# A fixed order of steps, engines and buffer slots in place of a planner, and a last batch cut into two token halves

## The chip, the cores and the metric

The kernel runs on one core of one Trainium2 chip. The metric is the time of one execution on the device in microseconds (us), smaller is better; the number compared is the median of several runs.

## What is computed

Two layers in a row, both attention. The first works on 4 batches of 8 heads with 768 tokens of 64 values: every token sees its neighbours closer than 16 tokens and a summary of each of the 24 blocks of 32 tokens (largest key, mean value). Its output, 4 batches of 768 tokens by 512 values, goes into four expert heads with causal attention; each token keeps its two best experts.

```python
# first layer, per batch and head
k_sum = k.reshape(B, H, nb, block, D).max(axis=3)
v_sum = v.reshape(B, H, nb, block, D).mean(axis=3)
scores_all = concat([where(|i - j| < 16, scale*q@k.T, -1e9), scale*q@k_sum.T + log(32)])
a = softmax(scores_all);  x = a @ concat([v, v_sum])
# second layer, per batch
logits = x @ w_gate;  topk = 2 best of 4;  w = softmax of the two
for e in range(4):
    q, k, v = x @ wq[e], x @ wk[e], x @ wv[e]
    a = softmax(causal(scale * q @ k.T))
    out += (e in topk) * w_e * (a @ v @ wo[e])
```

## The kernel before

A batch and two heads make a **pair**; there are 16, four to a batch. `stage1_pair` loads q, k and v of a pair, narrows q and k to 16 bits (`narrow`), turns them on TensorE (`turn`, `take`), takes the largest key of each block (`key_sums`), fills the value tile (`overlap`, `fill_rows`) and then does two halves of 384 tokens each: `scores`, `expo` (the exponential), `values`, `recip` and `norm`, `back` (turned back) and `take_hi`, `take_lo`, which keep the result as a 16-bit number and its remainder. The block means of v come from one more load for each batch (`load_vs`, tile `v_s`, 1536 KB), four additions that halve it each time (`fold`), a trip through DRAM (`park`, `fetch`) and one addition (`join`); no `values` of a batch can run before its `join`.

When the four pairs of a batch are done, `values_and_gate` makes the experts' values and the gate (`gate_a`, `gate_b`, `gate_exp`, `gate_c`), `experts(b, cc)` does two experts at a time: two projections, six units of scores with their exponentials, the causal cut on GpSimd (`causal`), the weighing in two parts (tokens 0 to 2 and 3 to 5, counted in tiles of 128), then `recip`, `comb`, `scale`, `turn` and `keep_t` for all six token tiles at once. `output` projects two token tiles at a time, copies them out of PSUM (`keep`) and stores them through GpSimd's queue (`store`).

Each such step is declared once with an engine (or several that could do it) and a cost. The order is not the order of declaration: `Plan.schedule` places step after step on the engine that can start one first, in the order of a priority made of a base time and an offset from the table `PO`, and hands out buffer slots as they come free. The emitted program is that order, and every engine works through its own list strictly in order. So a step that waits holds everything behind it on its engine, and SyncE, which issues all loads, holds all later loads while one waits for its slot.

Slots matter: two tiles each for the loaded q and k (`q_f`, `k_f`), three value tiles (`v_blk`), one `v_s`, two staging tiles for weights (`w_st`); in PSUM two tiles of one bank (`P1`) and three of two banks (`P2`).

Of the kernel before, what the change touches and what calls it, by code (L numbers as in the profile page):

```python
# [64 lines left out]
PO = {  # L65
    'const_ident': -11.677,
    'const_idt': 1.577,
    'const_mask': 33.311,
    'const_pads': 7.266,
    'experts.causal': 8.585,  # L70
    'experts.comb': -19.049,
    'experts.expo': -5.527,
    'experts.keep': 11.958,
    'experts.keep_t': 2.062,
    'experts.project': -0.122,
    'experts.recip': -4.407,
    'experts.scale': 11.954,
    'experts.scores': 4.304,
    'experts.turn': 18.467,
    'experts.weigh.go': 7.812,  # L80
    'output.keep': 15.877,
    'output.project': -32.546,
    'output.store': 2.114,
    'stage1_pair.back': -3.094,
    'stage1_pair.expo': -0.092,
    'stage1_pair.fetch': -2.828,
    'stage1_pair.fill_rows.go': 10.985,
    'stage1_pair.fold': 6.215,
    'stage1_pair.join': -10.17,
    'stage1_pair.key_sums': 5.122,  # L90
    'stage1_pair.load.go': 0.943,
    'stage1_pair.load_v': -0.911,
    'stage1_pair.load_vs': -6.414,
    'stage1_pair.narrow.go': 0.944,
    'stage1_pair.norm': -6.422,
    'stage1_pair.overlap.go': 3.015,
    'stage1_pair.park': -13.703,
    'stage1_pair.recip': 5.535,
    'stage1_pair.scores': -2.294,
    'stage1_pair.take.go': 2.871,  # L100
    'stage1_pair.take_hi': -17.93,
    'stage1_pair.take_lo': -13.515,
    'stage1_pair.turn.go': 0.229,
    'stage1_pair.values': -2.472,
    'values_and_gate.gate_a': 0.856,
    'values_and_gate.gate_b': -4.384,
    'values_and_gate.gate_c': -31.465,
    'values_and_gate.gate_exp': 2.173,
    'values_and_gate.keep': -9.634,
    'values_and_gate.keep_gate': 6.829,  # L110
    'values_and_gate.project': 2.576,
    'w_gate': 5.41,
    'w_keep_out.go': 16.522,
    'w_keep_qk.go': 29.21,
    'w_keep_v.go': -4.478,
    'w_load_gate': -0.971,
    'w_load_out.go': -3.109,
    'w_load_qk.go': -1.103,
    'w_load_v.go': -0.78,
    'warm.go': -10.334,  # L120
}
# [12 lines left out]
class Plan:
# [762 lines left out]
```

## Time and profile before

| | us |
|---|---|
| median of 3 runs | 211.81 (211.69 to 214.48) |
| the profiled execution, whole | 211.55 |
| its span, first to last instruction | 209.9 |
| TensorE busy | 170.9 |
| VectorE busy | 149.4 |
| ScalarE busy | 126.2 |
| GpSimd busy | 91.8 |

The span is what the trace shows; 1.65 us of the profiled execution lie outside it. PE is TensorE's matmuls, DVE is VectorE, ACT is ScalarE, POOL is GpSimd, SP is SyncE, which only issues transfers here. A stretch of the span in which no engine is full is one in which they wait for one another or for a transfer.

### The profile page before, as it was taken

How to read it: one execution, taken by the hardware profiler on the slowest of the kernel's cores; microseconds unless marked ns; L12 is line 12 of the kernel's file. 1: busy time of each engine (PE TensorE's matmuls, PEld its weight loads, DVE VectorE, ACT ScalarE, POOL GpSimd, SP SyncE). 2: the span in 40 equal slices, each digit the busy share in tenths (PEclk: the TensorE clock that was granted, in tenths of full speed). 3: DMA queues.
4: the chain of work that ended last, by engine and by line, in shares of the span. 5: the costliest groups of instructions: out<-in, count | busy, mean ns of one | idle time of the engine just before them, and what ended most of it. 6: DMA issues, size and time to landing. Idle time of an engine off the chain costs nothing. (4 is left out here: it accounts for less than half of the span.)

```text
span 209.9 us, 6029 instructions
## 1 busy us (share of the span) xinstructions
PE 170.9 (81%) x2488; PEld 122.9 (59%) x2488; DVE 149.4 (71%) x312; ACT 126.2 (60%) x168; POOL 91.8 (44%) x131
## 2 busy tenths in 40 slices
PE   7285978669999688998499996999999989958560
PEld 7153666447867456886265674786666676526420
DVE  5566777998978698878878896688694777603340
ACT  2266536666693997594438978367487754398010
POOL 3013638216563499689416954623411330443121
PEclk9999969999999999999969999999999999997578
DMA  6998999989999998999904996050430000600015
GB/s 213 306 230 194 239 336 154 220 186 252 291 220 263 306 219 178 251 315 228 206 19 129 363 215 86 3 78 2 169 134 3 3 5 0 268 34 3 0 59 241
DMA packets 45163, 34.73 MB, mean 166 GB/s; under 512 B 33360, under 2 KB 42832, under 8 KB 44624
## 3 DMA queue, kind: packets, MB, share of 16 engines
q1 hardware_dynamic: 43408, 28.07, 60.3%
q0 software_dynamic: 1728, 6.29, 7.5%
q8 instruction: 19, 0.31, 0.7%
q14 instruction: 8, 0.07, 0.1%
HBM read 27.66 MB, written 6.68 MB: 164 GB/s over the span
## 5 line engine op out<-in xcount | busy, mean ns | idle before, releaser
L758 ACT ACTIVATE a<-pb 128x1024 f16<-128x1024 f32 (+1 forms) x48 | 41.1, 933 | 7.0 <-PE pb L752 7.0
L606 PE MATMUL pa<-v_blk,aT 120*64 120x65 f32 x768 | 29.9, 234 | 5.1 <-DVE rec L615 2.0
L769 POOL TENSOR_SCALAR_AFFINE_SELECT a<-a 128x256 f16<-128x256 f16 x48 | 20.9, 449 | 29.5 <-ACT a L758 29.1
L594 ACT ACTIVATE aT<-pb 120x768 f32<-120x768 f32 x32 | 25.8, 814 | 11.3 <-PE pb L587 11.0
L606 PEld LDWEIGHTS pa<-v_blk,aT 120*64 120x64 f32 x768 | 26.4, 146 | 10.0 <-issue 2.5
L729 PE MATMUL pb<-hi,wqk 128*128 128x512 f16 (+1 forms) x128 | 24.2, 339 | 0.0
L526 POOL COPY v_blk<-v_blk 32x704 f32<-32x704 f32 x16 | 12.6, 794 | 26.3 <-DMA v_blk<-in_v_dram 26.2
L628 PE MATMUL pa<-ident,x 128*128 128x128 f32 x96 | 17.3, 293 | 7.0 <-DVE x L619 6.5
L638 DVE TENSOR_TENSOR lo<-pa,hi 128x384 f16<-128x384 f32 x32 | 17.7, 555 | 3.3 <-ACT hi L634 2.6
L519 POOL COPY v_blk<-vsum 24x768 f32<-24x768 f32 x20 | 17.8, 914 | 2.3 <-PE pa L606 1.7
L619 DVE TENSOR_TENSOR x<-pa,rec 128x384 f32<-128x384 f32 x32 | 17.8, 557 | 1.1
L845 POOL DMA_DIRECT2D out_dram<-o_sb x12 | 8.8, 737 | 22.3 <-DVE o_sb L842 9.0
L784 PE MATMUL pb<-v,a 128*128 128x65 f16 x336 | 14.9, 202 | 4.2 <-POOL a L769 3.3
L752 PE MATMUL pb<-qkT,qkT 64*128 64x512 f16 (+3 forms) x128 | 15.8, 321 | 2.9 <-ACT a L758 1.4
L729 PEld LDWEIGHTS <-wqk 128*128 128x128 f16 x128 | 12.5, 101 | 7.9 <-issue 1.0
L784 PEld LDWEIGHTS <-a 128*128 128x128 f16 x336 | 13.3, 103 | 6.4 <-POOL a L769 3.8
L628 PEld LDWEIGHTS pa<-ident,x 128*128 128x128 f32 x96 | 10.5, 145 | 10.8 <-DVE x L619 9.2
L582 PEld LDWEIGHTS <-kT 64*96 64x96 f16 x384 | 14.8, 129 | 2.7 <-issue 1.1
L559 DVE TENSOR_REDUCE ksum<-kT 128x24 f16<-128x768 f16 x16 | 15.2, 947 | 0.2
L582 PE MATMUL pb<-qT,kT 64*96 64x64 f16 x384 | 14.4, 211 | 0.8 <-ACT qT L548 0.8
L541 PE MATMUL pa<-ident,k_nat 128*128 128x128 f16 x96 | 9.0, 237 | 7.3 <-ACT k_nat L533 3.7
L489 POOL TENSOR_TENSOR v_s<-v_s 128x768 f32<-128x768 f32 (+1 forms) x5 | 12.3, 2459 | 4.5 <-DMA v_s<-in_v_dram 4.3
(91 smaller groups left out, 314.1 us busy)
## 6 DMA issues: line engine op xcount, KB each, us to landing
v_s<-in_v_dram SPq DMA_DIRECT2D x4, 1536.0 KB, 8.4
k_f<-in_k_dram SPq DMA_DIRECT2D x16, 384.0 KB, 5.8
q_f<-in_q_dram SPq DMA_DIRECT2D x16, 384.0 KB, 6.7
out_dram<-o_sb POOLq DMA_DIRECT2D x12, 512.0 KB, 4.0
v_blk<-in_v_dram SPq DMA_DIRECT2D x16, 288.0 KB, 7.3
v_blk<-in_v_dram SPq DMA_DIRECT2D x32, 44.0 KB, 6.0
w_st<-in_moe_wv_dram SPq DMA_DIRECT2D x4, 128.0 KB, 5.2
w_st<-in_moe_wq_dram SPq DMA_DIRECT2D x4, 128.0 KB, 5.1
```

Source lines behind the costliest of these rows:

```text
L519: copy(v_blk.ap[WIN:KR, hp, :, 0:64], vsum.ap[WIN:KR, 2 * c + hp, :].unsqueeze(1).to_broadcast((NSUM, NQ, 64)))
L582: nc.tensor.matmul(o[0:WIN, hp, 64 * t:64 * t + 64], kT.ap[rows[hp], g:g + WIN], qT.ap[rows[hp], g:g + 64], start=False, stop=(t == 5), sk ...
L594: nc.scalar.activation(aT.ap[0:KR], sc.ap.rearrange("p (h n) -> p h n", h=2)[0:KR, :, 0:384], AF.Exp, scale=SCALE)
L606: nc.tensor.matmul(o[64 * par:64 * par + 64, i, hp, :], aT.ap[0:KR, hp, 64 * t:64 * t + 64], v_blk.ap[0:KR, hp, 6 * u + t, 0:65], start=Tr ...
L619: nc.vector.tensor_tensor(x32.ap.rearrange("p i (h d) -> p i h d", h=2), o[:, :, :, 0:64], rec.ap.to_broadcast((128, 3, 2, 64)), AL.mult)
L628: nc.tensor.transpose(xT_ps.ap[:, 128 * i:128 * i + 128], x32.ap[:, i, :], ident32)
L638: nc.vector.tensor_tensor(lo.ap[:, cols], xT_ps.ap[:, 0:384], hi.ap[:, cols], AL.subtract)
L729: nc.tensor.matmul(pp.ap[:, lo:hi], wqk[:, ch, cc, j, :], xh[ch].ap[:, lo:hi], start=(ch == 0), stop=(ch == NCH - 1), skip_group_check=True)
L752: nc.tensor.matmul(o[:, ep, c:c + w], kT.ap[rows, 128 * tj:128 * tj + 128], qT.ap[rows, n0:n0 + w], start=True, stop=True, skip_group_chec ...
L758: nc.scalar.activation(a.ap[:, :, 0:ln], sp.ap.rearrange("p (e n) -> p e n", e=2)[:, :, 0:ln], AF.Exp, scale=SCALE / (XS * XS))
L769: nc.gpsimd.affine_select(dg, dg, [[0, 2], [1, 128]], AL.is_ge, 0.0, base=0, channel_multiplier=-1)
L784: nc.tensor.matmul(o[:, ep, ti, :], a2[u].ap[:, ep, c:c + 128], v2.ap[:, tj, 2 * cc + ep, :], start=(tj == 0), stop=(tj == ti), skip_group ...
```

## The change

The planner and its table of offsets go. In their place stands `ORDER`, a table with one entry for each step: its number in the order of declaration, a letter for the engine, and the slots of the buffers that it opens. `emit` goes through the table. The instructions of a step are the same as before, with these exceptions: the last batch's weighing, reciprocal, scaling, turning and copying are done for token tiles 0 to 2 and 3 to 5 apart, in one-bank PSUM tiles, and its output in four pieces (tiles 0 and 1; 2; 3 and 4; 5) and not three; the stores of the last two batches are issued by SyncE and not by GpSimd; `gate_c` is cut into three steps. The costs that stand beside the steps no longer decide anything.

```diff
-PO = {
-    'const_ident': -11.677,
...
+LETTER = {"P": "PE", "D": "DVE", "A": "ACT", "G": "POOL", "S": "SP"}
+ORDER = """
+0G 3D 6S0 83S0 8S0 1G 4P0 54S1 5S1 45S0 2D 17D0 19P10 43S 86D0 21A 88P00 90D 92D0 9D 143S0 57G1
...
-    def schedule(self):
...
     def emit(self):
-        for o in self.schedule():
+        steps = []
+        for step in ORDER.split():
+            n = next(i for i, ch in enumerate(step) if ch in LETTER)
+            o, eng, slots = self.ops[int(step[:n])], LETTER[step[n]], list(step[n + 1:])
             for b in o.bufs:
-                if b.ap is not None or b.tag is None:
-                    continue
-                b.ap = self.slots[b.tag][b.slot]
+                if b.owner is o and b.tag is not None:
+                    b.ap = self.slots[b.tag][int(slots.pop(0), 36)]
+            steps.append((o, eng))
+        for o, eng in steps:
             if o.table:
-                o.fn(o.table[o.eng])
+                o.fn(o.table[eng])
...
+        for tis in ((0, 1, 2), (3, 4, 5)) if b == B - 1 else ((0, 1, 2, 3, 4, 5),):
+            n, wide = len(tis), "P2" if len(tis) == NT else "P1"
+            wav, av2, r2, cmb = Buf("wav"), Buf(wide), Buf("rr"), Buf("rr")
...
+        for tis in ((0, 1), (2,), (3, 4), (5,)) if b == B - 1 else ((0, 1), (2, 3), (4, 5)):
+            n = len(tis)
+            op, o_sb = Buf("P2" if n == 2 else "P1"), Buf("o_sb")
...
+            late = b >= 2
+
+            def store(tis=tis, o_sb=o_sb, n=n, late=late):
+                (nc.sync if late else nc.gpsimd).dma_start(
```

Three places show what the table does. The first is SyncE at the start of the program, before and then after (`v_s` is the load for the block means, `q_f` and `k_f` are loads of q and k, `v_blk` the value tile in three parts, `vdram` the `park`, `w_st` weights for the experts' values, `wg_f` for the gate).

```order
L481 DMA v_s_116<-in_v_dram 128x3072
L445 DMA k_f_68<-in_k_dram 128x2x384
L445 DMA q_f_66<-in_q_dram 128x2x384
L462 DMA v_blk_113<-in_v_dram 48x24x64
L466 DMA v_blk_113<-in_v_dram 16x11x64 x2
L470 DMA v_blk_113<-in_v_dram 16x2x64
L445 DMA k_f_69<-in_k_dram 128x2x384
L445 DMA q_f_67<-in_q_dram 128x2x384
L499 DMA vdram_124<-vrow_117 128x192
```

After:

```order
L365 DMA q_f_66<-in_q_dram 128x2x384
L365 DMA k_f_68<-in_k_dram 128x2x384
L401 DMA v_s_116<-in_v_dram 128x3072
L365 DMA q_f_67<-in_q_dram 128x2x384
L365 DMA k_f_69<-in_k_dram 128x2x384
L300 DMA w_st_174<-in_moe_wv_dram 128x4x64 x4
L294 DMA wg_f_187<-in_moe_w_gate_dram 128x4x4
L365 DMA k_f_68<-in_k_dram 128x2x384
L365 DMA q_f_66<-in_q_dram 128x2x384
L365 DMA q_f_67<-in_q_dram 128x2x384
L382 DMA v_blk_113<-in_v_dram 48x24x64
L386 DMA v_blk_113<-in_v_dram 16x11x64 x2
```

The first value tile stood fourth on SyncE and now stands behind seven loads of q and k, the block-mean load and two loads of weights; the seven are of pairs 0 to 3 of batch 0 and one of batch 1.

The second place is SyncE at the first load of the experts' query and key weights (`w_st` from `in_moe_wq` and `in_moe_wk`), before and then after.

```order
L374 DMA wg_f_187<-in_moe_w_gate_dram 128x4x4
L380 DMA w_st_174<-in_moe_wv_dram 128x4x64 x4
L445 DMA k_f_68<-in_k_dram 128x2x384
L445 DMA q_f_66<-in_q_dram 128x2x384
L462 DMA v_blk_114<-in_v_dram 48x24x64
L466 DMA v_blk_114<-in_v_dram 16x11x64 x2
L470 DMA v_blk_114<-in_v_dram 16x2x64
L400 DMA w_st_175<-in_moe_wq_dram 128x4x64
```

After:

```order
L419 DMA vdram_125<-vrow_118 128x192
L401 DMA v_s_116<-in_v_dram 128x3072
L382 DMA v_blk_114<-in_v_dram 48x24x64
L386 DMA v_blk_114<-in_v_dram 16x11x64 x2
L390 DMA v_blk_114<-in_v_dram 16x2x64
L365 DMA k_f_69<-in_k_dram 128x2x384
L423 DMA vhalf_119<-vdram_125 24x8x128
L365 DMA q_f_67<-in_q_dram 128x2x384
L320 DMA w_st_174<-in_moe_wq_dram 128x4x64
```

That load was in row 32 of SyncE's list and is now in row 45; ahead of it stand 19 loads of q or k where there were 10, three of `v_s` where there were two, and the output weights (512 KB). Value tiles ahead of it are five in both.

The third place is ScalarE at the start of the last batch's exponentials (`a` from `pb` is an expert unit's exponential, `qkT` a projection's copy, `o_sb` an output copy of batch 2), before and then after.

```order
L735 CAST qkT_142<-pb_64 128x768
L703 ACTIVATE gtmp_135<-gtmp_136 128x24
L842 COPY o_sb_177<-pb_63 128x1024
L842 COPY o_sb_178<-pb_64 128x1024
L758 ACTIVATE a_146<-pb_65 128x1024
L758 ACTIVATE a_147<-pb_63 128x1024
```

After:

```order
L623 ACTIVATE gtmp_135<-gtmp_136 128x24
L661 CAST qkT_145<-pb_64 128x768
L661 CAST qkT_143<-pb_65 128x768
L684 ACTIVATE a_147<-pb_64 128x1024
L684 ACTIVATE a_148<-pb_65 128x1024
L684 ACTIVATE a_149<-pb_64 128x1024
L684 ACTIVATE a_152<-pb_63 128x2x128
L684 ACTIVATE a_153<-pb_65 128x1024
L684 ACTIVATE a_154<-pb_64 128x1024
L777 COPY o_sb_177<-pb_64 128x1024
L684 ACTIVATE a_146<-pb_65 128x1024
```

The output of batch 2 stood ahead of all twelve exponentials of the last batch and now stands between the two groups of six.

## Rows read from the trace of the kernel before

**Rows 1.** The page's busy times: us, share of the span, instructions

```profile
PE 170.9 (81%) x2488; PEld 122.9 (59%) x2488; DVE 149.4 (71%) x312; ACT 126.2 (60%) x168; POOL 91.8 (44%) x131
```

**Rows 2.** Busy us (instructions) of each engine by stretch; then granted clock, DMA share, GB/s

```profile
core 0: us, PE busy (x) PEld busy (x) DVE busy (x) ACT busy (x) POOL busy (x), PEclk, DMA share, GB/s
0.00:65.70 65.70, 50.39 (x716) 38.57 (x718) 50.49 (x116) 36.83 (x50) 26.09 (x34) 0.97 1.07 235
65.70:168.60 102.90, 92.48 (x1486) 66.83 (x1486) 81.79 (x161) 72.17 (x97) 55.10 (x77) 0.98 0.64 157
100.00:105.00 5.00, 1.88 (x12) 0.97 (x10) 4.23 (x14) 2.48 (x4) 2.10 (x2) 1.00 1.07 200
105.00:110.00 5.00, 4.98 (x22) 3.02 (x23) 3.83 (x8) 2.05 (x3) 0.76 (x1) 0.66 0.06 17
...
194.50:209.90 15.40, 6.50 (x45) 3.41 (x45) 4.37 (x6) 1.06 (x2) 2.78 (x5) 0.73 0.25 102
```

**Rows 3.** Timeline of VectorE and GpSimd, 96 to 103 us: start, duration, instruction

```profile
96.86 5.32 POOL L489 TENSOR_TENSOR v_s<-v_s 128x1536 f32<-128x1536 f32 x2 [0.20 <-DMA v_s<-in_v_dram]
...
98.50 1.84 DVE L689 SCALAR_TENSOR_TENSOR gtmp<-lgp 128x24 f32<-128x24 f32 x1
...
100.59 1.64 DVE L692 TENSOR_TENSOR gtmp<-gtmp,small 128x24 f32<-128x24 f32 x1
102.15 0.17 DVE L697 TENSOR_TENSOR gtmp<-gtmp,small 128x24 f32<-128x24 f32 x1
```

**Rows 4.** Timeline: first users of loads, 14 to 46 us, idle time before in brackets

```profile
14.23 0.56 DVE L533 CAST k_nat<-k_f 128x768 f16<-128x768 f32 x1 [1.32 <-DMA k_f<-in_k_dram]
...
15.22 0.56 DVE L533 CAST q_nat<-q_f 128x768 f16<-128x768 f32 x1 [0.43 <-DMA q_f<-in_q_dram]
...
27.36 0.83 ACT L533 CAST q_nat<-q_f 128x768 f16<-128x768 f32 x1 [0.18 <-DMA q_f<-in_q_dram]
...
31.98 3.42 POOL L489 TENSOR_TENSOR v_s<-v_s 128x1536 f32<-128x1536 f32 x1 [4.14 <-DMA v_s<-in_v_dram]
...
45.31 1.04 ACT L406 CAST wqk<-w_st 128x1024 f16<-128x1024 f32 x1 [1.16 <-DMA w_st<-in_moe_wk_dram]
```

**Rows 5.** TensorE's timeline: units of work, one of them in the dip of the clock

```profile
61.41 2.76 PE L729 MATMUL pb<-hi,wqk 128*128 128x512 f16 x16
64.11 1.62 PE L606 MATMUL pa<-v_blk,aT 120*64 120x65 f32 x48
...
66.47 0.88 PE L628 MATMUL pa<-ident,x 128*128 128x128 f32 x6
...
105.40 2.05 PE L729 MATMUL pb<-hi,wqk 128*128 128x512 f16 x8
...
171.44 1.08 PE L784 MATMUL pb<-v,a 128*128 128x65 f16 x30
```

**Rows 6.** Timeline of GpSimd and TensorE at 128 to 131 us

```profile
128.03 0.76 POOL L526 COPY v_blk<-v_blk 32x704 f32<-32x704 f32 x1 [2.13 <-DMA v_blk<-in_v_dram]
...
130.56 0.39 PE L784 MATMUL pb<-v,a 128*128 128x65 f16 x7 [1.87 <-POOL a L769]
```

**Rows 7.** Timeline of the tail, all engines, 176 us to the end

```profile
176.19 2.75 PE L837 MATMUL pb<-wo_cat,wT 128*128 128x512 f16 x12
...
183.25 4.96 ACT L758 ACTIVATE a<-pb 128x1024 f16<-128x1024 f32 x6 [3.21 <-PE pb L752]
...
197.02 0.96 DVE L807 TENSOR_TENSOR wav<-pb,rr 128x768 f16<-128x768 f32 x1
...
199.51 3.62 PE L837 MATMUL pb<-wo_cat,wT 128*128 128x512 f16 x11 [0.23 <-DVE wT L822]
...
203.16 1.23 DVE L842 COPY o_sb<-pb 128x1024 f32<-128x1024 f32 x1 [0.88 <-PE pb L837]
...
204.69 0.72 POOL L845 DMA_DIRECT2D out_dram<-o_sb  x1 [0.31 <-DVE o_sb L842]
```

**Rows 8.** The page's transfers: KB each, median us from issue to landing

```profile
out_dram<-o_sb POOLq DMA_DIRECT2D x12, 512.0 KB, 4.0
```

More of the change, by code (lines that the diff above doesn't have):

```diff
@@ L55 @@
 VP = 128
-PAIR0, PAIR1, S2OFF, S2B, S2P, NHI, NLO, WP = 5.835, 6.633, 4.705, 31.197, 4.325, 12, 8, 14.749
-DELTA = 0
-BIAS = {'ACT': 0.0, 'DVE': -0.013, 'POOL': 0.126}
+PAIR0, PAIR1, S2OFF, S2B, S2P, VGO, NHI, NLO, WP = 6.0, 6.6, 0.0, 33.0, 6.0, 0.0, 12, 8, 14.0
 COPY = {}
 ADD = {}
-PO = {
-    'const_ident': -11.677,
[L67 to L121, printed above, removed]
@@ L127, in __init__ @@
-        self.ap, self.owner, self.last, self.since = None, None, 0.0, 0.0
+        self.tag, self.writers, self.ap, self.owner = tag, [], None, None
 class Op:
-    __slots__ = ("eng", "cost", "fn", "bufs", "deps", "prio", "end", "alts", "start", "lat", "table", "idx")
+    __slots__ = ("fn", "bufs", "deps", "prio", "alts", "lat", "table", "idx", "dma")
 class Plan:
-    LAT = {"PE": 0.20, "DVE": 0.12, "ACT": 0.16, "POOL": 0.16, "SP": 0.0}
     def __init__(self):
@@ L335, in const_mask @@
                                     base=31, channel_multiplier=1)
-    P.op("POOL", 2.0, const_mask, w=[C_msk], prio=-90)
+    P.op("POOL", 2.4, const_mask, w=[C_msk], prio=-90)
     def const_idt():
@@ L509, in join @@
                 add(vsum.ap[WIN:KR], vhalf.ap[WIN:KR, :, 0, :], vhalf.ap[WIN:KR, :, 1, :], AL.add)
-            P.op("SP", 0.5, park, r=[vrow], w=[d_row], prio=-4.0, lat=2.0)
-            P.op("SP", 0.6, fetch, r=[d_row], w=[vhalf], prio=-3.5, lat=2.0)
-            P.op({"DVE": 0.65, "POOL": 1.2}, 0, join, r=[vhalf], w=[vsum], prio=-3.5, table=ADD)
+            P.op("SP", 0.45, park, r=[vrow], w=[d_row], prio=-4.0, dma=(1, 0.3))
+            P.op("SP", 0.45, fetch, r=[d_row], w=[vhalf], prio=-3.5, dma=(1, 0.5))
+            P.op({"DVE": 0.69, "POOL": 1.3}, 0, join, r=[vhalf], w=[vsum], prio=-3.5, table=ADD)
             st["vs"] = vsum
@@ L770, in causal @@
                                                 base=0, channel_multiplier=-1)
[L771 removed]
+                    P.op("POOL", 0.45, causal, r=[a], w=[a])
                 c += w
             a2.append(a)
[L774 to L788 removed]
@@ L859 @@
     for b in range(B):
-        for i, part in enumerate((lambda: values_and_gate(b), lambda: experts(b, 0),
-                                  lambda: experts(b, 1), lambda: output(b))):
-            P.base = PAIR0 * NCH + S2OFF + S2B * b + S2P * i
-            part()
+        for part, off in ((values_and_gate, VGO), (lambda b: experts(b, 0), S2P),
+                          (lambda b: experts(b, 1), 2 * S2P), (output, 3 * S2P)):
+            P.base = PAIR0 * NCH + S2OFF + S2B * b + off
+            part(b)
     with tc.manual_schedule():
```

313 lines of the change are left out of this document (150 added, 163 removed).

## The prediction

> **What bounds the kernel now.** I read the page's busy times first [rows 1]: no engine is full. TensorE is busy 170.9 of 209.9 us, VectorE 149.4. So the question is where TensorE waits, and the busy times by stretch answer it [rows 2]. Up to 65.7 us TensorE is busy 50.4 of 65.7, and the transfers are the full resource (DMA share 1.07, 235 GB/s). From 65.7 to 168.6 us, from the scores of batch 1's third pair to the last `back` of the last pair, TensorE is busy 92.5 of 102.9 and VectorE 81.8; that is the steady part. From 168.6 us there is only the end of batch 2 and the last batch, 41.3 us. The chain of waits names only the last stores here, so I work by these three stretches.
>
> In the steady part two holes stand out. From 100 to 105 us TensorE is busy 1.9 of 5 and from 105 to 110 us, after that idling, its granted clock averages 0.66, part of it at the lower of its two levels, 1.2 GHz [rows 2]; VectorE was sitting in two gate instructions of 1.84 and 1.64 us, while a like one beside them takes 0.17 [rows 3]. At 130.6 us TensorE waited 1.87 us for a causal cut on GpSimd, which had stood 2.13 us at a value tile's load [rows 6].
>
> In the tail, the twelve exponentials of the last batch begin at 183.25 us, 14.6 us after the last `back`, and the last store is issued at 204.69, 5.2 us before the end [rows 7].
>
> **The change, first stretch: weights later.** TensorE can't pass its first expert projection, since it is in order, and that waits for the experts' query and key weights. Before, their landing released a cast at 45.31 us [rows 4]. After, the same load stands behind nine more loads of q or k, one more `v_s` load, the output weights and one more `park` and `fetch`. A q load landed 0.99 us after the k load ahead of it (14.23 to 15.22), and a `v_s` load 4.62 us after the q load ahead of it (27.36 to 31.98) [rows 4]. So: 9 x 0.99 = 8.9, plus 4.6, plus 512 KB of output weights at the q rate (0.99 x 512 / 384 = 1.3), plus two small transfers of 96 KB (0.5 by the same rate): 15.3 us, landing at 60.6. The upper bound takes the mean rate of the first 65.7 us instead: these loads are 5.8 MB, at 235 GB/s 24.8 us, landing at 70.1 [rows 2]. I take 62.5, near the lower end, because these are long-run loads like those two rows. The cast moves from ScalarE to GpSimd; with 1.04 us before [rows 4] and some of GpSimd's own list (narrowing, filling) ahead of it, 1.5 us. TensorE starts its first expert projection at **64.0**.
>
> That is no loss by itself. Before 65.7 us the old order had done more: its remaining list from there to the last `back` is the 102.9 us stretch. The new list from its first expert projection to the last `back` holds the same kinds of step and a few more: four expert projections (1.38 each, two in 2.76: 5.5), two `values` (0.81, two in 1.62: 1.6), one `back` (0.44), and one second part of weighing fewer (1.08) [rows 5]; one unit of expert scores more and one turn fewer cancel. Net 6.5 us more. The early prefetch of q and k brings nothing by itself: batch 0's values come later, and TensorE has little to do until 64.
>
> **Second stretch.** At the old pace: 102.9 + 6.5 = 109.4 us. Off that comes what the new order doesn't repeat. The hole at 100: 3.1 us idle, and two projections at the low clock, of which one took 2.05 in place of 1.38 (0.67 each, 1.3): 4.4 us. Its gate steps (batch 1) stand after the fourth batch's folds in the new table, behind a projection of their own, so they don't meet. The hole at 130: 1.9 us; the copies that wait for loads now stand farther ahead of the causal cuts. So 109.4 - 4.4 - 1.9 = 103.1, and the last `back` ends at 64.0 + 103.1 = **167.1** (168.6 before). The other 8 us or so of waits I leave: VectorE gets more to do (ten casts of q and k in place of seven, 22 `take_hi` in place of 16, nine output copies in place of five, against 14 `take` in place of 20), and both engines are nearly full there, so a denser order of TensorE has little to lean on.
>
> **Third stretch, the tail.** Up to the first exponential of the last batch: before 14.6 us. The output projection of batch 2 (12 matmuls, 2.75 us [rows 7]) and one of four expert projections (1.38) move behind the first scores, and 0.5 us of weighing's second part with them: 14.6 - 2.75 - 1.38 - 0.5 = 10.0. The exponentials took 11.3 us (183.25 to 194.5, ScalarE without a pause worth naming). One output copy now stands between the two groups of six (1.23 us on VectorE for the same size [rows 7], about 1.0 here), and ScalarE waits for the moved projections for part of 2.75 us, say 0.8: 13.1. After the last exponential: 15.4 us before [rows 2], as weighing to 196.5, scaling to 198.0, turning and copying to 199.5, output matmuls 3.62 to 203.1, copy 1.23 to 204.4, store and end 5.5. The halves take off: scaling 0.4 (half of 0.96), turning and copying 0.3, the six matmuls of tiles 0 to 2 that run while VectorE scales the second half, and a last copy of half the size, less the two copies that now follow one another on VectorE: 3.6 + 1.25 becomes 1.3 + 1.23 + 0.7, so 1.6. The store is half as large and issued by SyncE: between no gain and 2.5 us off (the whole 4.0 us from issue to landing of a 512 KB store [rows 8] can't go), I take 1.2. So 15.4 - 0.4 - 0.3 - 1.6 - 1.2 = 11.9. Tail 10.0 + 13.1 + 11.9 = **35.0** in place of 41.3. The move of the stores to SyncE's queue costs nothing, since all loads stand ahead of them there and have long landed.
>
> **Sum.** Span 64.0 + 103.1 + 35.0 = 202.1. Outside the span 1.65, so 203.75 beside a profiled execution of 211.55; the median of the runs is 0.26 above that: **204.0 us**, 3.7% less. About 2% (4.2 us) is what a measurement of this kernel can tell from no change.
>
> **Rivals.**
>
> *The old pace stays.* VectorE is the reason: 81.8 busy of 102.9 us beside TensorE's 92.5 [rows 2], and more copies come to it. Then nothing comes off the 109.4: 64.0 + 109.4 + 35.0 = 208.4, time 210.3. No change that can be measured. Against it: the two holes have a cause that the new order moves.
>
> *VectorE meets GpSimd's folds again, in another place.* In the new order the third batch's two folds run on GpSimd just ahead of the weights' cast, and VectorE has at that place `join`, `overlap` and batch 0's first gate step. The row shows what such a meeting costs: (1.84 - 0.17) + (1.64 - 0.17) = 3.1 us on VectorE during a 5.32 us pair of folds [rows 3], and TensorE's idle 3.1 us in the same stretch [rows 2] followed from it. Here that would go straight into the start at 64.0: 204.0 + 3.1 = 207.1. The Trainium skill (SBUF — State Buffer, section on two separate sides) says that VectorE and GpSimd share one pair of ports as an exclusive lock: a VectorE instruction with two SBUF inputs, or in a fast mode that takes both ports, and a GpSimd one block each other for a whole instruction. The stretched rows agree, both having two SBUF inputs; by that rule every fold on GpSimd (six in the new table, five in the old) is a trap for a gate step, a `join` or an SBUF copy beside it. Without the rule the same instruction costs 0.17 and the sum stays at 204.0.
>
> *The weights are the loss.* If loads keep the mean rate of the first stretch, the weights land at 70.1, the projections start at 71.6, and with nothing gained in the pace the span is 71.6 + 109.4 + 35.0 = 216.0, time 217.9: slower by 2.9%. For it: the new order loads q of batch 2 among its first twenty loads, which is of no use for 50 us, and small value loads still stand between. At the old pace the change loses from a start of 65.5 on, and measurably (216.0 us) from 69.7. Against it: the two differences in [rows 4] are of the very loads that were moved ahead.
>
> *Denser than I think.* If TensorE's idle 10.4 us (102.9 - 92.5) all went, with the slow clock's 1.3: 102.9 - 10.4 - 1.3 + 6.5 = 97.7, and 64.0 + 97.7 + 34.0 + 1.9 = 197.6. For it: the new order hands out slots with full knowledge of what follows. It needs VectorE's waits to be gone too.
>
> **How the numbers follow.** Forecast (204.0, by the unknowns of landing, tail and store 201 to 208): 0.45. Meeting of folds (207.1): 0.11. Old pace (210.3): 0.20. Late weights (216 to 218): 0.11. Denser (197.6): 0.13. The range leaves out the late weights and the last part of the dense case: 197.5 to 213. Faster by over 2% (below 207.6): most of the forecast (0.39), the dense case (0.13), over half of the fold case (0.06) and little of the old pace (0.02): 0.60. Slower by over 2% (above 216.0): most of the late weights: 0.10. Within: 0.30.
>
> **What the new profile would show.** Right: the first cast of the experts' weights released by a load at 61 to 64 us; TensorE's first expert projection at about 64; the last `back` at about 167; the first exponential of the last batch 10 us after that and the end 12 us after the last one. Wrong, if the cast waits for GpSimd's folds and not for the load; if VectorE shows waits in the steady part where TensorE did; if the output copies of the last batch queue up on VectorE and the store takes its 5 us still. The prediction fails altogether if the fixed order holds an engine at a step whose input comes late by some microseconds, again and again, since nothing can overtake it; the place to look at is TensorE's idle time between 64 and 167, which I put at some 5 us (10.4 less the two holes' 3.1 and 1.9).

## The result and the profile after

The median went from 211.75 to 203.49 us (202.89 to 204.49), a ratio of 0.963 with a 95% interval of 0.957 to 0.969. The profiled execution took 202.89 us, its span 201.2.

The page's busy times, to be read beside [rows 1]:

```profile
PE 164.9 (82%) x2488; PEld 119.2 (59%) x2488; DVE 156.0 (78%) x327; ACT 121.4 (60%) x160; POOL 92.3 (46%) x127
```

TensorE has the same number of instructions and 6 us less busy time. By stretch (the columns are those of [rows 2]): up to the first expert projection, to the last `back`, to the last batch's first exponential, to the end of its last one, to the end.

```profile
0.00:69.90 69.90, 43.29 (x637) 34.05 (x638) 51.54 (x113) 29.95 (x40) 29.87 (x32) 0.80 1.01 249
69.90:168.50 98.60, 96.87 (x1543) 69.53 (x1541) 84.33 (x168) 75.23 (x99) 56.72 (x82) 0.99 0.63 144
168.50:177.60 9.10, 9.10 (x124) 6.79 (x121) 6.48 (x22) 3.98 (x7) 0.94 (x3) 1.00 0.01 2
177.60:191.00 13.40, 11.48 (x150) 6.59 (x147) 9.34 (x19) 11.14 (x14) 4.19 (x11) 1.00 0.31 117
191.00:201.20 10.20, 4.19 (x48) 2.25 (x48) 4.35 (x8) 1.09 (x3) 0.59 (x2) 0.88 0.40 156
```

The last `back` ends at 168.45 us, where it ended before (168.6). The first projection comes 22.1 us later than before (69.9; 47.8 in the trace of before), the way from there to the last `back` is 22.3 us shorter (98.5 and 120.9): these two cancel. The tail is 32.8 us and not 41.3, and that is the whole gain. In the long middle TensorE idles 1.7 us, all of it before 105 us; from there to 165 us none:

```profile
105.00:165.00 60.00, 60.00 (x979) 43.86 (x975) 49.79 (x107) 47.10 (x63) 29.25 (x46) 1.00 0.48 124
```

Before 105 us a fold on GpSimd meets a step of VectorE (`comb`) once, and TensorE waits for that step's result:

```profile
96.22 3.43 POOL L409 TENSOR_TENSOR v_s<-v_s 128x1536 f32<-128x1536 f32 x1
...
97.77 1.93 DVE L735 TENSOR_TENSOR rr<-rr,gate 128x12 f32<-128x12 f32 x1
...
100.74 0.51 PE L751 MATMUL pa<-ident,wav 128*128 128x128 f16 x6 [1.15 <-DVE wav L739]
```

The place at which the prediction had the first projection at 64.0 (timeline of all engines, 55 to 72 us; compare [rows 3, 4]):

```profile
55.21 5.33 POOL L409 TENSOR_TENSOR v_s<-v_s 128x1536 f32<-128x1536 f32 x2 [1.54 <-DVE rec L535]
...
63.02 0.82 POOL L439 COPY v_blk<-vsum 24x768 f32<-24x768 f32 x1 [2.49 <-DVE vsum L429]
...
64.32 0.69 DVE L609 SCALAR_TENSOR_TENSOR gtmp<-lgp 128x24 f32<-128x24 f32 x1
...
65.91 0.76 DVE L618 SCALAR_TENSOR_TENSOR gtmp<-gtmp,gtmp 128x24 f32<-128x24 f32 x1
...
66.70 1.04 POOL L326 CAST wqk<-w_st 128x1024 f16<-128x1024 f32 x1
...
66.91 0.86 DVE L620 TENSOR_TENSOR gtmp<-gtmp,small 128x24 f32<-128x24 f32 x1
...
68.52 0.50 PE L461 MATMUL pa<-ident,q_nat 128*128 128x128 f16 x6 [1.69 <-DVE x L539]
...
69.91 2.55 PE L655 MATMUL pb<-hi,wqk 128*128 128x512 f16 x7
```

The cast of the weights (66.70) shows no wait for a transfer: GpSimd came to it late, behind a fill that waited for `join` and behind two narrowings. TensorE then waited 1.69 us for VectorE, four of whose gate steps took 0.52 to 0.86 us while GpSimd worked beside them.

The tail, ScalarE's and VectorE's rows and the store (compare [rows 7, 8]):

```profile
177.62 1.02 ACT L684 ACTIVATE a<-pb 128x1024 f16<-128x1024 f32 x1
178.96 4.05 ACT L684 ACTIVATE a<-pb 128x1024 f16<-128x1024 f32 x5 [0.32 <-PE pb L678]
184.58 1.01 ACT L777 COPY o_sb<-pb 128x1024 f32<-128x1024 f32 x1 [1.57 <-PE pb L772]
185.77 1.94 ACT L684 ACTIVATE a<-pb 128x1024 f16<-128x1024 f32 x2 [0.18 <-PE pb L678]
187.90 3.13 ACT L684 ACTIVATE a<-pb 128x1024 f16<-128x1024 f32 x4 [0.19 <-PE pb L678]
...
193.41 4.07 SPq L782 DMA_DIRECT2D out_dram<-o_sb  x4
...
196.42 0.68 DVE L777 COPY o_sb<-pa 128x512 f32<-128x512 f32 x1
```

The last copy ends at 197.1, the span 4.1 us later; before, 5.5 us lay between (204.4 to 209.9).

The experiments below are read by stage, from their own traces, in us. Of the profiled executions marked * no total is read, since they were up to 4% longer than the runs that the ratios compare.

| kernel | first `values` | first projection | to last `back` | to first exponential | exponentials | to the end |
|---|---|---|---|---|---|---|
| before | 21.5 | 47.8 | 120.9 | 14.6 | 11.3 | 15.4 |
| changed | 32.3 | 69.9 | 98.5 | 9.2 | 13.4 | 10.2 |
| GpSimd's stores | 33.1 | 71.8 | 98.5 | 9.2 | 13.4 | 10.9 |
| no halves | 32.8 | 69.9 | 101.0 | 9.2 | 14.4 | 13.2 |
| batch 2's output first * | 33.5 | 73.5 | 99.7 | 16.3 | 12.1 | 10.2 |
| all three * | 33.6 | 70.6 | 101.9 | 16.3 | 12.5 | 15.2 |
| value tiles early * | 32.9 | 77.4 | 102.8 | 9.2 | 13.4 | 11.7 |
| gate and cast moved * | 32.1 | 71.6 | 101.4 | 9.2 | 13.4 | 10.1 |
| no `take_lo` | 33.5 | 71.1 | 96.0 | 9.2 | 13.4 | 10.1 |
| no gate remainder | 32.9 | 70.8 | 97.1 | 8.6 | 13.4 | 10.2 |
| changed, once more * | 32.3 | 71.6 | 103.1 | 9.2 | 13.4 | 11.8 |
| three steps moved | 33.3 | 70.1 | 100.7 | 9.2 | 13.4 | 10.1 |
| means first * | 28.5 | 76.5 | 102.2 | 9.2 | 13.4 | 11.8 |
| values first | 24.3 | 74.1 | 101.8 | 9.2 | 13.4 | 10.2 |

Up to the last `back` the changed kernel, GpSimd's stores and no halves have one and the same order of steps, and yet they differ by 1.9 us at the first projection and by 2.5 us behind it. A difference of that size between two other rows shows nothing by itself. The stages of the tail repeat to 0.1 us in the rows without * whose edits leave them alone.

### The profile page after: what moved, and what is told of

Same layout as the page of the kernel before. It is cut to its first block, busy times and chain, and to the rows that moved or that the text cites. A ratio compares the mean times of both kernels' runs of the same rounds, so it can differ in the third digit from the quotient of the medians.

```text
span 201.2 us, 6032 instructions
## 1 busy us (share of the span) xinstructions
PE 164.9 (82%) x2488; PEld 119.2 (59%) x2488; DVE 156.0 (78%) x327; ACT 121.4 (60%) x160; POOL 92.3 (46%) x127
## 4 chain that ended last, share of the span: by engine, by line
PE 58%; DMA 12%; DVE 12%; SPq 7%; issue 3%; POOL 3%; ACT 2%; DVEq 1%; POOLq 0%
PE pa L526 10%; PE pb L655 9%; DMA v_blk<-in_v_dram 9%; PE pa L548 6%; PE pb L579 5%; PE pb L772 5%; PE pb L678 4%; SPq L300 4%; PE pa L461 3%; PE pb L717 3%; PE pb L496 3%; DMA vhalf<-vdram 3%; PE pb L507 3%; PE pb L502 3%; DVE wav L739 2%
## 5 line engine op out<-in xcount | busy, mean ns | idle before, releaser
L684 ACT ACTIVATE a<-pb 128x1024 f16<-128x1024 f32 (+1 forms) x48 | 41.3, 922 | 4.3 <-PE pb L678 4.1
L526 PE MATMUL pa<-v_blk,aT 120*64 120x65 f32 x768 | 30.2, 234 | 10.2 <-ACT v_blk L439 8.0
L695 POOL TENSOR_SCALAR_AFFINE_SELECT a<-a 128x256 f16<-128x256 f16 x48 | 19.6, 415 | 35.8 <-ACT a L684 35.3
L446 POOL COPY v_blk<-v_blk 32x704 f32<-32x704 f32 x16 | 12.5, 789 | 22.5 <-DMA v_blk<-in_v_dram 22.2
L439 POOL COPY v_blk<-vsum 24x768 f32<-24x768 f32 x16 | 14.7, 927 | 10.8 <-PE pa L526 6.6
L539 DVE TENSOR_TENSOR x<-pa,rec 128x384 f32<-128x384 f32 x32 | 17.8, 558 | 1.1
L409 POOL TENSOR_TENSOR v_s<-v_s 128x1536 f32<-128x1536 f32 (+1 forms) x6 | 15.7, 2622 | 4.5 <-DMA v_s<-in_v_dram 2.7
L468 ACT COPY qT<-pa 128x768 f16<-128x768 f16 x11 | 8.8, 802 | 13.8 <-PE pa L461 13.8
L554 DVE CAST hi<-pa 128x384 f16<-128x384 f32 x22 | 12.2, 554 | 5.3 <-PE pa L548 5.0
L461 PE MATMUL pa<-ident,q_nat 128*128 128x128 f16 x96 | 8.7, 231 | 9.1 <-POOL q_nat L453 6.8
L678 PE MATMUL pb<-qkT,qkT 64*128 64x512 f16 (+3 forms) x128 | 15.4, 309 | 0.6 <-DVE wav L739 0.6
L453 POOL CAST q_nat<-q_f 128x768 f16<-128x768 f32 x9 | 8.1, 900 | 15.0 <-DMA q_f<-in_q_dram 5.9
L548 PEld LDWEIGHTS pa<-ident,x 128*128 128x128 f32 x96 | 10.9, 148 | 6.4 <-DVE x L539 3.6
```

What stands on the lines that cost most here:

```text
L409: add(t[:, :, 0:half] if half > 64 else vrow.ap, t[:, :, 0:half], t[:, :, half:2 * half], AL.add)
L526: nc.tensor.matmul(o[64 * par:64 * par + 64, i, hp, :], aT.ap[0:KR, hp, 64 * t:64 * t + 64], v_blk.ap[0:KR, hp, 6 * u + t, 0:65], start=Tr ...
L539: nc.vector.tensor_tensor(x32.ap.rearrange("p i (h d) -> p i h d", h=2), o[:, :, :, 0:64], rec.ap.to_broadcast((128, 3, 2, 64)), AL.mult)
L548: nc.tensor.transpose(xT_ps.ap[:, 128 * i:128 * i + 128], x32.ap[:, i, :], ident32)
L678: nc.tensor.matmul(o[:, ep, c:c + w], kT.ap[rows, 128 * tj:128 * tj + 128], qT.ap[rows, n0:n0 + w], start=True, stop=True, skip_group_chec ...
L684: nc.scalar.activation(a.ap[:, :, 0:ln], sp.ap.rearrange("p (e n) -> p e n", e=2)[:, :, 0:ln], AF.Exp, scale=SCALE / (XS * XS))
```

## Where the gain lies: the tail

The theory is that the tail alone makes the difference; the rival, that the denser middle does and the tail's edits are small.

**GpSimd's stores.**

```diff
-                (nc.sync if late else nc.gpsimd).dma_start(
+                nc.gpsimd.dma_start(
```

> The changed kernel with one thing undone: the stores of the last two batches are issued by GpSimd again, at the same places in the order. Theory (the gain lies in the tail, 41.3 us before and 32.8 after, while the last back ends at 168.5 in both): the end after the last copy grows from 4.1 us to the 5.5 us of before, and the causal cuts of the last six units stand behind three stores on GpSimd, so 1.5 to 3 us slower than the changed kernel, 205.0 to 206.5 us. Rival (the gain is the denser steady stretch, and the edits in the tail are worth little each): within 0.5 us of 203.5.

Ratio 0.971 (0.960 to 0.983), against 0.963: 1.7 us more, within the theory's range, but the intervals overlap. The stage says more: 10.9 us behind the last exponential in place of 10.2, and nothing elsewhere in the tail. SyncE's stores are worth 0.7 us.

**No halves.**

```diff
-        for tis in ((0, 1, 2), (3, 4, 5)) if b == B - 1 else ((0, 1, 2, 3, 4, 5),):
+        for tis in ((0, 1, 2, 3, 4, 5),):
...
-        for tis in ((0, 1), (2,), (3, 4), (5,)) if b == B - 1 else ((0, 1), (2, 3), (4, 5)):
+        for tis in ((0, 1), (2, 3), (4, 5)):
```

> The changed kernel without the token halves: the last batch's weighing, scaling and turning for six token tiles at once, its output in three pieces, everything else in the same order. Theory of the tail: the terms of the prediction for the halves come back, 0.4 + 0.3 + 1.6 = 2.3 us, so 205.8 us (205 to 206.5). Rival of the steady stretch: 203.5 to 204.0.

Ratio 0.987 (0.980 to 0.994): 2.5% slower than the changed kernel, twice what was expected. Behind the last exponential it takes 13.2 us (3.0 more), and the exponentials 1.0 more. That part lies in waits: the weighing stood 0.69 us until a copy of batch 2's output freed a two-bank tile, and the last scores stand behind a turn that waited 0.99 us for VectorE's scaling.

```profile
189.18 1.44 PE L715 MATMUL pb<-v,a 128*128 128x65 f16 x42 [0.69 <-DVE o_sb L775]
...
192.15 0.51 PE L749 MATMUL pa<-ident,wav 128*128 128x128 f16 x6 [0.99 <-DVE wav L737]
```

Windows and timeline of this kernel, from the last exponential:

```profile
194.43:207.60 13.17, 6.06 (x43) 2.59 (x40) 4.37 (x6) 1.01 (x1) 0.56 (x2) 0.79 0.31 119
```

```profile
198.47 4.24 PE L770 MATMUL pb<-wo_cat,wT 128*128 128x512 f16 x11 [0.44 <-DVE wT L752]
```

The eleven matmuls run at 0.385 us each; the changed kernel's four of tiles 0 and 1 took 1.03 together, 0.26 each. TensorE had idled before them, and the granted clock of the stretch averages 0.79 here and 0.88 in the changed kernel. Whether the halves keep the clock up isn't shown by that: with halves the average lay between 0.80 (three steps moved, for the same busy time) and 0.96.

**Batch 2's output first.** On ScalarE (steps by name, batch and experts):

```diff
 ex[3,1]keep.j0
+out[2]keep.(2,3)
 ex[3,0]expo.u3
...
 ex[3,0]expo.u2
-out[2]keep.(2,3)
 ex[3,1]expo.u2
```

> The changed kernel with batch 2's output (its matmuls, copies and stores) and the fourth projection ahead of the last batch's exponentials again. Theory of the tail: the first exponential comes 2.75 + 1.38 = 4.1 us later, and of that 1 to 2 us come back because ScalarE no longer pauses between the two groups of six: 2 to 3 us slower, 205.5 to 206.5. Rival of the steady stretch: 203.5 to 204.5.

Ratio 0.998 (0.992 to 1.003): three and a half per cent slower than the changed kernel, more than either theory had. The first exponential comes 16.3 us behind the last `back`, 7.1 later, and 1.3 of that comes back, as was expected. It is 1.7 later even than in the kernel before, for the edit moved more on TensorE than the output: ahead of the first scores there are now the 12 output matmuls, a projection (1.3), the rest of the weighing (0.9), two turns (0.8) and two waits, of 1.20 us for VectorE's scaling and 0.24 for a copy. Timeline, and the stretch up to the first exponential:

```profile
184.40 0.51 PE L749 MATMUL pa<-ident,wav 128*128 128x128 f16 x6 [1.20 <-DVE wav L737]
...
186.05 2.75 PE L770 MATMUL pb<-wo_cat,wT 128*128 128x512 f16 x12
```

```profile
173.21:189.53 16.32, 14.89 (x184) 10.39 (x181) 11.74 (x30) 5.10 (x9) 0.98 (x3) 1.00 0.02 6
```

The clock has no part in this delay: it is granted at 1.00 all through. In the exponentials' stretch that follows it is not:

```profile
189.53:201.66 12.13, 8.07 (x88) 4.42 (x85) 3.90 (x12) 10.09 (x12) 4.21 (x11) 0.72 0.33 125
```

TensorE has 8.1 us of work there (11.5 in the changed kernel) and its clock averages 0.72 in place of 1.00.

**All three.** The three edits together.

> All three at once: GpSimd's stores, no halves, batch 2's output first; the order up to the last back is the changed kernel's. Theory of the tail: the whole gain goes, 203.5 + 8.5 = 212 us (210.5 to 212.5), no faster than the kernel before. Rival of the steady stretch: the kernel stays well ahead of the one before, below 207.

Ratio 1.015 (1.006 to 1.025): nothing of the gain is left, with the first 170 us as the table has them. The tail takes 44.0 us, 11.2 more than the changed kernel's, and the parts nearly add up to it (0.7 + 4.0 + 5.8 = 10.5). It is also 2.7 us longer than the 41.3 of the kernel before, so the edits, that of batch 2's output above all, undo somewhat more than the change did. The rival falls. Its windows, by the three stages:

```profile
172.57:188.90 16.33, 14.90 (x184) 10.40 (x181) 11.76 (x30) 5.11 (x9) 1.83 (x5) 1.00 0.00 1
188.90:201.40 12.50, 8.64 (x96) 5.19 (x93) 2.46 (x5) 10.03 (x12) 5.55 (x13) 0.63 0.32 128
201.40:216.60 15.20, 6.90 (x44) 3.32 (x41) 4.38 (x6) 1.01 (x2) 2.73 (x5) 0.61 0.25 103
```

## What bounds the middle: VectorE or TensorE

**No `take_lo`.** The remainder is zeroed once at the start.

```diff
-                nc.vector.tensor_tensor(lo.ap[:, cols], xT_ps.ap[:, 0:384], hi.ap[:, cols],
-                                        AL.subtract)
+                pass
```

> The changed kernel without take_lo: the 32 subtractions that make the remainder of the 16-bit numbers (17.9 us on VectorE) are left out and the remainder is zero, set once at the start. TensorE's work is the same. Theory (TensorE is the bound from 105 to 177, VectorE is not, though 86 per cent busy): only the idle time of TensorE from 70 to 105, 1.7 us, and some of the wait before can go, 1 to 2.5 us faster, 201 to 202.5. Rival (VectorE sets the pace): 5 us faster or more, below 198.5.

Ratio 0.949 (0.938 to 0.959), 1.5% or 3 us below the changed kernel's, for some 17.8 us of VectorE's work; the two intervals overlap. Its middle is 96.0 us, 2.5 less, which is no more than one order varies. From 105 to 165 us VectorE is busy 43.1 where it was 49.8, and TensorE the same:

```profile
105.00:165.00 60.00, 60.00 (x986) 44.19 (x986) 43.06 (x96) 47.03 (x63) 30.54 (x48) 1.00 0.49 122
```

The size lies just past the theory's range and short of the rival's. The firm part is the stretch: with 6.7 us less on VectorE, TensorE is busy all through in both kernels, so VectorE does not set the pace behind 105 us.

**No gate remainder.**

```diff
-                        nc.tensor.matmul(vp.ap[:, o:o + 264], xh[ch].ap[:, cols], wvg[:, ch, :],
-                                         start=(ch == 0), stop=False, skip_group_check=True)
-                    for ch in range(NCH):
-                        nc.tensor.matmul(vp.ap[:, o + 256:o + 264], xl[ch].ap[:, cols],
-                                         wvg[:, ch, 256:264],
-                                         start=False, stop=(ch == NCH - 1), skip_group_check=True)
+                        nc.tensor.matmul(vp.ap[:, o:o + 264], xh[ch].ap[:, cols], wvg[:, ch, :],
+                                         start=(ch == 0), stop=(ch == NCH - 1),
+                                         skip_group_check=True)
```

> The changed kernel without the gate's matmuls on the remainder (24 groups of four matmuls at 0.25 us, 6.0 us of TensorE in all, 4.5 of them after its first expert projection); the gate is then computed from the 16-bit numbers alone. VectorE's work is the same. Theory (TensorE is the bound): 4 to 4.5 us faster, 199.0 to 199.5. Rival (VectorE or the transfers set the pace): within 1 us of 203.5.

Ratio 0.949 (0.933 to 0.964), about 3 us less, between the two; its interval overlaps the changed kernel's. The price was wrong. In the changed kernel a token tile's two groups lie so:

```profile
170.76 0.61 PE L579 MATMUL pb<-wvg,hi 128*128 128x264 f16 x4
171.21 0.24 PE L582 MATMUL pb<-wvg,lo 128*128 128x8 f16 x4
171.31 0.61 PE L579 MATMUL pb<-wvg,hi 128*128 128x264 f16 x4
```

The next tile starts 0.55 us after the first, though the durations add up to 0.85. Without the small group (the row of this kernel) four tiles take 1.90 us to the next instruction, 0.475 each:

```profile
60.02 1.96 PE L577 MATMUL pb<-wvg,hi 128*128 128x264 f16 x16
```

So 24 groups are worth 24 x 0.08 = 1.9 us, not 6.0, and the 18 of them behind the first projection 1.4. The middle and the stretch behind it are 1.4 and 0.6 us shorter. The 0.6 is what the six groups there give; the 1.4 and the rest of the 3 us are within what one order varies. The run therefore bears the theory out only weakly.

## What sets the start

**Gate and cast moved.** GpSimd, then VectorE:

```diff
 s1[2,0]fold.256
+w_keep_qk
 s1[1,0]fill_rows.h1
...
 s1[1,1]fill_rows.h1
-w_keep_qk
```

```diff
 s1[1,0]fill_rows.h0
-vg[0]gate_a
-vg[0]gate_b
 s1[1,0]recip.u1
...
 s1[1,0]norm.u0
+vg[0]gate_a
+vg[0]gate_b
```

> The changed kernel with four steps moved near 66 us: batch 0's first two gate steps go behind the reciprocals and products of batch 1's first pair on VectorE, and the cast of the first query and key weights goes directly behind the folds on GpSimd. Theory (not the load but GpSimd's list and the gate steps that VectorE did beside GpSimd's copies held the first projection at 69.9; the weights had landed by about 63.5): the first projection at 67 to 68, and the end 2 us earlier, 201.5. Rival (loads of the value tiles at 79 to 91 us set the pace next and eat the gain): the first projection at 67 to 68 and the time within 0.7 of 203.5.

It has one time to compare, 202.48 us, and so no interval. With the gate's first steps `gate_exp` moved too, on ScalarE, behind a fill. The first projection is at 71.6, not at 67: the expectation fell, and the trace says why.

```profile
64.40 1.04 POOL L324 CAST wqk<-w_st 128x1024 f16<-128x1024 f32 x1 [2.98 <-DMA w_st<-in_moe_wk_dram]
65.50 0.83 POOL L437 COPY v_blk<-vsum 24x768 f32<-24x768 f32 x1
...
69.86 0.17 DVE L607 SCALAR_TENSOR_TENSOR gtmp<-lgp 128x24 f32<-128x24 f32 x1
```

Now the cast waits for its transfer, which lands at 64.4, 4.2 us after its last issue ended (60.16). By that the weights of the changed kernel, issued to 59.62, landed at about 63.8. And the cast, standing first, held the fill that `values` need. The gate steps, away from GpSimd's copies, take 0.17 to 0.18 us each; four of them had taken 2.8 together: 2.1 us of stretching, that is the meeting of the two engines.

**Value tiles early**, on SyncE:

```diff
 s1[0,0]load k_f
-w_load_v
-w_load_gate
+s1[0,0]load_v
+s1[0,1]load_v
 s1[1,0]load k_f
```

> The changed kernel with another order at the start: on SyncE the first two value tiles go ahead of the values' weights and the gate's, which move behind the third value tile, the fetch goes two loads earlier, and on VectorE the first join stands ahead of the second pair's overlap. Theory (TensorE is the bound from about 70 us on, without idle time from 105 to 177, so an earlier start comes out at the end): the first values move from 32.3 to about 26 us, the first expert projection from 69.9 to 66 or 67, the time to 200 to 201.5. Rival (the transfers are the bound until 70 us, at a share of 1.01, and their bytes are the same): the first values come earlier, the first projection does not, 203.5 give or take 1.

Ratio 0.984 (0.971 to 0.997): slower than the changed kernel by 2%, on the wrong side of both. The first `values` stay at 32.9, where I had looked for 26. `park` was issued at 19.06, `fetch` at 25.35, and `join` ran at 31.26. I took this for a wait on the block means' trip through DRAM, and the next run rests on it, but that isn't shown: SyncE did wait 3.9 us for `park` before it issued `fetch`, while `join` came directly behind VectorE's step before it, and VectorE had waited 2.26, 0.23 and 1.18 us for loads of q and k since 22.9 us. The edit also put the casts of the values' and the gate's weights behind other steps of GpSimd and VectorE.

**Means first.** The `v_s` load, `park` and `fetch` ahead on SyncE:

```diff
+s1[0,0]load_vs
 s1[0,0]load q_f
 s1[0,2]load k_f
-s1[0,0]load_vs
 s1[0,1]load q_f
 s1[0,0]load k_f
-w_load_v
-w_load_gate
+s1[0,0]load_v
+s1[0,0]park
+s1[0,1]load_v
+s1[0,0]fetch
 s1[1,0]load k_f
```

> The changed kernel with the block means' path first: the v_s load first on SyncE as in the kernel before, its folds first on VectorE, then the first value tile, the park, the second value tile and the fetch ahead of the far q and k loads; the values' weights and the gate's behind the third value tile; join and the first fills ahead of the second pair's steps. Theory (the first values wait for the trip of the block means through DRAM behind a full queue, 17.0 to 30.7 us): first values at 23 to 25 us in place of 32.3 to 33.6, and since TensorE is full from about 75 us on, what is left of that at the first projection comes out at the end: 2 to 5 us less than the changed kernel. Rival (the transfers of the first 64 us are the bound and SyncE's list now holds the far loads later): the first values earlier, the first projection not earlier or later, the time the same or up to 6 us more, as in the run with early value tiles.

Ratio 0.997 (0.992 to 1.002). `values` come 3.9 us earlier, the first projection 6.6 later. GpSimd shows one cause, which is a fault of my order: it stood at the values' weights ahead of batch 1's folds, so `park` came at 54.48 (47.87 in the changed kernel), and all later loads behind it.

```profile
40.28 1.04 POOL L304 CAST wvg<-w_st 128x1024 f16<-128x1024 f32 x1 [9.33 <-DMA w_st<-in_moe_wv_dram]
```

**Values first.** The same with both casts behind the folds, batch 0's `values` ahead of the next q and k, and the three steps of the run below.

> The three moved steps of the run before, and the block means' path first as in the run with the means first, but without the two faults that its trace showed: there GpSimd stood 9.3 us at the values' weights ahead of batch 1's folds, and VectorE 3.0 us at the gate's weights, and SyncE's later loads queued up behind the park of those folds. Now both casts stand behind the folds, the far q load (batch 2, second pair) goes behind the first two loads of query and key weights, and batch 0's first overlap, join, fills and values stand ahead of the second and third pair's q and k. Theory (an earlier start comes out at the end as long as SyncE's list is not held): first values at 22 to 25 us, batch 1's park before 46, first projection at 63 to 67, the time 199 to 202 us, or 0.94 to 0.955 of the kernel before. Rival (the transfers up to 64 us are the bound, whatever the order): first values early, first projection at 69 to 71, the time as in the run with three moved steps, 0.96 to 0.97.

Ratio 1.005 (0.999 to 1.012). The first `values` are at 24.3, as expected, 8 us ahead of the changed kernel; the first projection is at 74.1, 4.2 us behind it. Both theories fall. What happened stands on SyncE, the transfers and GpSimd (one of SyncE's waits: us in total, times, longest; busy times 20 to 30 us; timeline):

```profile
SPq L363 <- DVE q_nat L451: 5.5, 1, 5.5
```

```profile
20.00:30.00 10.00, 5.87 (x70) 4.58 (x69) 5.72 (x12) 3.67 (x5) 2.42 (x3) 0.50 0.40 135
```

```profile
38.55 5.50 POOL L407 TENSOR_TENSOR v_s<-v_s 128x1536 f32<-128x1536 f32 x2 [12.92 <-DMA v_s<-in_v_dram]
```

SyncE waited 5.5 us for a q slot, because the narrowing that frees it now stood behind `values` on VectorE; the transfers fell to a share of 0.40, batch 1's `v_s` landed 2 us later, and the weights were issued from 61.1 and not 55.1. The first projection itself didn't wait for those weights: their cast at 68.24 shows no wait. It stood behind batch 1's fill, on which TensorE waited 3.45 us, and that behind a `join` of 2.12 us (0.69 in the changed kernel) beside a fold whose load had come late.

```profile
61.23 5.44 POOL L407 TENSOR_TENSOR v_s<-v_s 128x1536 f32<-128x1536 f32 x2 [5.34 <-DMA v_s<-in_v_dram]
...
65.11 2.12 DVE L427 TENSOR_TENSOR vsum<-vhalf 24x512 f32<-24x512 f32 x1
...
68.69 2.87 PE L524 MATMUL pa<-v_blk,aT 120*64 120x65 f32 x48 [3.45 <-ACT v_blk L437]
```

Here, without the early loads of q and k, the transfers paused. Bytes and share up to 55 us, before, changed, means first and values first:

```profile
0.00:55.00 55.00, 39.69 (x549) 30.63 (x549) 41.41 (x92) 28.61 (x37) 19.53 (x25) 0.97 1.05 233
```

```profile
0.00:55.00 55.00, 31.32 (x432) 24.12 (x434) 39.40 (x85) 20.43 (x26) 19.29 (x24) 0.75 1.01 266
```

```profile
0.00:55.00 55.00, 32.77 (x342) 24.36 (x343) 36.84 (x76) 17.79 (x23) 15.74 (x22) 0.91 0.89 231
```

```profile
0.00:55.00 55.00, 36.96 (x396) 27.59 (x396) 35.62 (x81) 19.93 (x26) 16.61 (x23) 0.63 0.87 243
```

266 GB/s are 1.8 MB more in 55 us than 233. The ten profiles with the changed kernel's order of loads have 248 to 266 GB/s, issue the weights from 55.1 to 59.0 us on and have the first projection at 69.9 to 73.5. The three with values or their tiles moved up have 231 (value tiles early), 231 and 243 GB/s, issue the weights from 61.1 to 63.0 on and have the first projection at 74.1 to 77.4. That the early loads of q and k alone make this difference is not shown, since each of the three edits moved other steps as well. Nothing of it is caught up again: the middle is no shorter than in the others.

**The base again, and three steps moved.** The cast behind the first fill, the gate as above, and the very last copy on ScalarE (the table's entry 866).

```diff
-866D
+866A
```

> The changed kernel as it is, as a base on the chip on which the next two run. Every theory: 0.963 of the kernel before, within its interval of 0.957 to 0.969.

> The changed kernel with three places moved: the very last output copy goes from VectorE to ScalarE (which has nothing left to do by then), batch 0's first two gate steps go behind batch 1's first reciprocals and products on VectorE, and the cast of the first query and key weights goes behind GpSimd's first fill, ahead of two narrowings and a fill. Theory: after the last exponential 9.4 us in place of 10.2 (the copy ran at 196.42 behind another of 1.22 us on VectorE and takes 0.58 on ScalarE), and the first projection 1.5 us after the weights have landed and the values' products are out, 68.2 in place of 69.9, which passes on to the end: 2.5 us less than the changed kernel on the same chip, 0.7 from the tail alone. Rival (what is gained at the start is lost at the next loads): 0.7 to 1 us less, all of it after the last exponential.

On one chip the changed kernel had 0.970 (0.962 to 0.978) and the three steps 0.964 (0.957 to 0.971), 0.6% or 1.3 us less, but the intervals overlap; the two stand level as far as this tells. The first projection is at 70.1 and 36.8 us behind the first `values`, where it was 37.6 (37.1 to 38.7 in the four other rows without * that start alike): the start shows no gain that could be told, where 1.7 was expected. The steps did act: from batch 1's `values` to the first projection 3.05 us passed (67.08 to 70.13) in place of 5.5 (64.39 to 69.91). But those `values` came 2.7 us later, behind a `join` at 64.89 and not 62.20, in a part of the order that the edit left alone. Behind the last exponential 0.1 us came of the 0.7:

```profile
197.62 1.23 DVE L775 COPY o_sb<-pb 128x1024 f32<-128x1024 f32 x1 [0.34 <-PE pb L770]
198.04 0.59 ACT L775 COPY o_sb<-pa 128x512 f32<-128x512 f32 x1 [1.39 <-PE pa L770]
```

The half-size copy now ends first, at 198.63, and the last store to be released is one of 512 KB: 4.65 us from its copy's end (198.85) to the end of the span, where the half-size one took 4.1.

## Why the prediction came out

The time was forecast at 204.0 and is 203.5. The tail's edits worked in the way that was said; that the number is so close is partly luck, since the errors of the other two stages went against each other.

- **Start at 64.0: mis-sized by 5.9 us** (69.9). The landing was right within about 1.3 us (62.5 forecast, some 63.8). The 1.5 us for GpSimd was the term that failed: its cast ended at 67.7, behind a fill that waited for VectorE's `join` and two narrowings (2.4 us of the 5.9). The last 2.2 us came behind the cast, where TensorE waited for VectorE, whose gate steps were stretched by 2.1 us. So a sign that I had named for being wrong was there: GpSimd's list released the cast and not the load. The rival of the meeting engines took place, at GpSimd's copies and not its folds, and not alone. The rule of the Trainium skill (SBUF — State Buffer, section on two separate sides) that I set against the sum agrees: four gate steps took 0.52 to 0.86 us beside GpSimd and 0.17 to 0.18 us in the run in which they stood elsewhere. At the folds, as that rival had it, the meeting came in the run with values first (`join`, 2.12 us).
- **"The early prefetch of q and k brings nothing by itself": not borne out.** Three orders that gave the value path precedence moved fewer bytes up to 55 us and had the first projection at 74.1 to 77.4 us, beyond the 69.9 to 73.5 of the ten others. What the prefetch alone is worth wasn't isolated.
- **Middle 103.1: mis-sized by 4.6 us** (98.5). Both holes went as forecast, except that a fold met VectorE once more at 97.8 us (`comb`, a step of 1.93 us, then 1.15 us of idle TensorE). What failed is "the other 8 us or so of waits I leave": the sum left TensorE 5.4 us of idle time, and 1.7 came; the other 0.9 is work (97.7 busy by the sum, 96.9 measured). The reason given, VectorE's load, failed with it: VectorE was busy 84.3 of 98.6 us, where it had been 81.8 of 102.9, and TensorE waited less all the same.
- **Tail 35.0: 32.8.** First exponential 9.2 (10.0), exponentials 13.4 (13.1), the rest 10.2 (11.9). Of the terms, the halves were worth 4.0 us where 2.3 were put, 1.0 of it in the exponentials through the waits shown above and 0.6 at the output matmuls (eleven in 4.24 us, where the price came from 3.62 in [rows 7]). SyncE's stores were worth 0.7 where 1.2 were put. Batch 2's output behind the scores was undone for 5.8 us net where 2.8 were put, but that edit moved more than the term; from before to changed the two stages that it bears on went from 25.9 to 22.6 us, 3.3 net.

The sum came out (202.1 and 201.2) because +5.9, -4.6 and -2.2 nearly cancel. Of the rivals, the old pace (109.4 for the middle) did not happen. "Late weights" has the start nearly right (71.6), but by a landing at 70.1 and not some 63.8. "Denser" has the middle nearly right (97.7), with the start at 64.0; its sum takes 34.0 for the tail, and with the 35.0 that was worked out it comes to 198.6.

Open: why one order of steps took 98.5, 98.5 and 101.0 us for the middle (100.7 with three steps moved, 99.7 to 103.1 in the rows marked *). The difference lies in TensorE's idle time and clock between 70 and 110 us, where transfers still run at shares of 0.6 to 1.3; which of them decides wasn't found. So how much of the middle's 98.5 belongs to the order is open, and so is whether the three steps are a gain.

## What to carry to other kernels

Work out the end of a kernel, where no other work covers a wait, as its own stage: this whole change was worth what it did to the last 41 us. While transfers are full, look at whether the issuing queue ever stops, and not only at how early the first consumer starts: the three orders here that favoured it began the next stage later. Profile one order several times before reading a stage to a microsecond or two. Price matmuls that are taken out or added by the distance between starts, not by their durations.

## What was not expected of the hardware

- **Issue of small-row loads.** Four loads of 128 KB for the values' weights (rows of 64 numbers) held SyncE for 7.31 us at 3.30 us in the changed kernel (5.13 before, at 29.50; 4.16 and 4.41 in the runs with value tiles early and with values first, later still); two loads of a value tile in their place held it for 7.07.
- **A small transfer behind full queues.** From the issue of `park` (96 KB) to the issue of the `fetch` that waits for it 6.3 us passed in the run with value tiles early (19.06, 25.35); SyncE stood waiting for it for 3.9 of them.
- **The clock in the tail.** 1.00 through the last batch's exponentials with batch 2's output between them; 0.72, 0.63 and, in the kernel before, 0.85 (183.25 to 194.54 us) with that output ahead of them, for the same twelve exponentials.
